# Feed-forward token blocks of 512 and 256 in place of 464 and 448, with x at another address

## The chip, the core and the metric

The kernel is one program on one core of a Trainium2 chip. The metric is the device time of one execution in microseconds (us), as the median of three runs. Beside it stands one execution that the hardware profiler recorded, with its own time and its span from the first to the last instruction.

## What is computed

Causal attention with a decay, on 4 batches of 8 heads with 576 positions and 64 features each, gives an array x of 2304 tokens by 512 features. Two feed-forward parts follow, both over all tokens:

```python
x = attention(q, k, v, f)            # 2304 tokens x 512
h = x @ moe_w_in                     # 512 -> 2048
x = (h * sigmoid(h)) @ moe_w_out     # 2048 -> 512
a, b = x @ moe2_w_a, x @ moe2_w_b    # 512 -> 1536, twice
out = (a * b) @ moe2_w_out           # 1536 -> 512
```

Inputs and output are float32.

## The kernel before

The program has two stretches. In the first, a planner (class `Plan`) orders the attention of 16 head pairs together with the first piece of the first feed-forward part, by hand-given durations and priorities; `first_chunk` is that piece, in token blocks of 288 columns (`NB`). Nothing in it reads `BLOCKS`.

The second stretch, the loops at the end of `model_kernel`, is the rest of both feed-forward parts. `chunk_layout` cuts the hidden features into 13 pieces, called chunks: `CH1` holds seven for the first part, `CH2` six for the second, with 1 to 3 tiles of 128 hidden features each. Chunk 0 is the one done in the first stretch; chunks 1 to 12 run here. For each chunk the loop goes over the token blocks of `BLOCKS`: four of 464 and one of 448.

- `ff_in(c, t, t0, n)` makes the hidden tile t for the n tokens from t0. `project` multiplies four 128-feature pieces of x (index kc) by the weights into one PSUM tile `ps`; in the second part there are two such tiles, for a and for b. ScalarE and VectorE turn it into g and split g into a high part `ghi` (line 342) and a low part `glo` (line 343).
- `ff_out(c, oc, t0, n)` multiplies `ghi` and `glo` by the second weights into a PSUM tile `po` and adds that to the accumulator `acc` (`add_out`, lines 364 and 373). The accumulator is held in two halves of 1152 tokens (`TAIL`), so the block that lies across token 1152 is added in two pieces.
- Every product is done by `mm3` as three matmuls with float32r operands (lines 310, 311, 312): high by high, high by low, low by high. The moving operand is a row of n columns of x or of g; the stationary operand is a 128 x 128 piece of the weights, loaded anew for each matmul.
- The loop writes `ff_in` of a block, then `ff_out` of the block before it. A scheduler of the framework sets the final order of the instructions on each engine from its own model.
- Meanwhile the weights of the next chunk are decoded (`decode`, lines 272 to 281) in pieces of 256 columns, three pieces (`PER`) after each token block: a load on SP, six passes on ScalarE and VectorE, two on GpSimd.
- In the last chunk `add_out` issues the output's DMA (line 375) after each add.

x is one tile of 128 partitions, [P, 2, KC, NT] float32r: index 0 of the second axis is the high part, 1 the low part, KC is 4, NT is 2304. In the built kernel it begins at byte 20,768 of each partition, which is 81 x 256 + 32. A step of kc is 9,216 bytes and from high to low 36,864 bytes, both multiples of 256, so what a block's read begins at, modulo 256, is (32 + 4 t0) modulo 256: 32, 96, 160 and 224 for the blocks at tokens 0, 464, 928 and 1392, and 32 for the one at 1856. It is set by the small tiles that stand ahead of x in a partition, of which `warm` ([NH, 1], 4 bytes, line 247) is the last: it only takes the result of an early Exp.

Of the kernel before, what the change touches and what calls it, by code (L numbers as in the profile page):

```python
# [9 lines left out]
F32 = mybir.dt.float32  # L10
# [3 lines left out]
AF = mybir.ActivationFunctionType  # L14
# [6 lines left out]
NT, DM = B * S, H * D  # L21
KC = DM // P
FF1, FF2 = 2048, 1536
NH = B * H
# [15 lines left out]


TAIL = NT // 2
BLOCKS = [(t, min(464, NT - t)) for t in range(0, NT, 464)]

# [183 lines left out]
def model_kernel(ctx: ExitStack, tc: tile.TileContext, qk, q0, v, f, w, out):  # L230
    nc = tc.nc
    chunks, _ = chunk_layout()

    const = ctx.enter_context(tc.tile_pool(name="const", bufs=1))
# [9 lines left out]
    dec = dram.tile([NH, 6, 2, S], BF16, name="dec")  # L244

    invs = dram.tile([NH // 2, 9, P], F32, name="invs")
    warm = const.tile([NH, 1], F32, name="warm")
    temp = ExitStack()
    dp = temp.enter_context(tc.tile_pool(name="dp", bufs=1))
    ft, one, cum = (dp.tile([NH, S], F32, name=n) for n in ("ft", "one", "cum"))  # L250
# [65 lines left out]
    gp = [None, 0, 0]  # L316
# [74 lines left out]
    plan = Plan()  # L391
# [3 lines left out]
    def buf(pool, tag, shape, dtype, name):  # L395
        n = SLOTS[tag]
        return Buf(tags[tag], lambda: (pool or dpool[0]).tile(shape, dtype, name=name, tag=tag, bufs=n))
# [6 lines left out]
    def prepare():  # L404

        pr = -9
        for n, (t, base, fill, op) in enumerate(((maskb, 0.0, MASKED, ALU.is_ge), (ident, 1.0, 0.0, ALU.is_equal))):
            plan.add("POOL", 142, lambda t=t, base=base: nc.gpsimd.memset(t, base), (), [("const", n)], -10)
            plan.add("POOL", 244, lambda t=t, fill=fill, op=op: nc.gpsimd.affine_select(
                t, t, pattern=[[-1, P]], compare_op=op, fill=fill, base=0, channel_multiplier=1), (), [("const", n)], -10)  # L410
        plan.add("DVE", 135, lambda: nc.vector.tensor_copy(identb, ident), [("const", 1)], [("const", 2)], pr)

        idle = warmth.append(buf(mm, "mm", [P, 512], F32, "idle")) or warmth[0]

        def run_up():
            for n in range(RUN_UP):
                nc.tensor.matmul(idle()[:, :P], identb, maskb, start=n == 0, stop=n == RUN_UP - 1)

        plan.add("PE", 6000, run_up, [("const", 0), ("const", 2)], [idle], pr)
        plan.dma(480, 74000, lambda: nc.sync.dma_start(ft, f), (), ["f"], pr)  # L420
        plan.add("DVE", 607, lambda: nc.vector.memset(one, 1.0), (), ["one"], pr)
        plan.add("DVE", 369, lambda: nc.vector.tensor_scalar(ft, ft, 1e-4, 1.0, ALU.max, ALU.min), (), ["f"], pr)
        plan.add("ACT", 1900, lambda: nc.scalar.activation(ft, ft, AF.Ln), (), ["f"], pr)

        plan.add("ACT", 1400, lambda: nc.scalar.activation(warm, one[:, 0:1], AF.Exp), ["one", "f"], ["warm"], pr)
        plan.add("DVE", 669, lambda: nc.vector.tensor_tensor_scan(cum, one, ft, 0.0, ALU.mult, ALU.add), ["f", "one"], ["cum"], pr)
        plan.add("POOL", 133, lambda: nc.gpsimd.tensor_copy(warm, cum[:, 0:1]), ["cum"], ["warm", "go"], pr)
        plan.add("DVE", 400, lambda: nc.vector.memset(maskw, 0.0), ["cum"], [("const", 3)], -7)
        plan.add("DVE", 250, lambda: nc.vector.memset(mask2, 0.0), ["cum"], [("const", 3)], -7)
        plan.add("POOL", 250, lambda: nc.gpsimd.tensor_copy(maskw[:, -P:], maskb), [("const", 0), "cum"], [("const", 3)], -7)  # L430
        for i in range(2):
            plan.add("POOL", 100, lambda i=i: nc.gpsimd.tensor_copy(mask2[i * D:(i + 1) * D, -D:], maskb[:D, :D]),
                     [("const", 0), "cum"], [("const", 3)], -7)
        for i, value in enumerate((-1 / SCALE, 1 / SCALE)):
            plan.add("POOL", 1200, lambda i=i, value=value: nc.gpsimd.memset(rows_sb[:, 3 - 3 * i:6 - 3 * i, i], value), ["cum"], [("rows", "const", i)], -8)
        rest = (ft, one)
        for n in range(3):
            src = cum if n == 0 else rest[n - 1]
            plan.add("DVE", 450, lambda n=n, src=src: nc.vector.tensor_copy(rows_sb[:, n, 0], src), [("c", n), "cum"], [("rows", n)], -8)
            if n < 2:  # L440
                plan.add("DVE", 750, lambda n=n, src=src: nc.vector.tensor_sub(rest[n], src, rows_sb[:, n, 0]),
                         [("c", n), ("rows", n), "cum"], [("c", n + 1), ("f", "one")[n]], -8)
        for n in range(3):
            plan.add("ACT", 530, lambda n=n: nc.scalar.copy(rows_sb[:, 3 + n, 1], rows_sb[:, n, 0]), [("rows", n)], [("rows", "k", n)], -8)
        plan.dma(480, 442000, lambda: nc.scalar.dma_start(dec, rows_sb), [("rows", n) for n in range(3)] + [("rows", "k", n) for n in range(3)] + [("rows", "const", i) for i in range(2)],
                 ["dec"], pr, eng="ACT")
# [338 lines left out]
    def keep_warm(order):  # L785
# [10 lines left out]
        return res  # L796

    prepare()
    fill_decays()

# [45 lines left out]


    mmpool[0] = ctx.enter_context(tc.tile_pool(name="mmB", bufs=8, space=PSUM))
    gp[:] = ctx.enter_context(tc.tile_pool(name="gB", bufs=2)), 3, 464
    prev = []  # L850
    for c in range(1, len(chunks)):
        pend = []
        for t0, nb in BLOCKS:
            for t in range(chunks[c][2]):
# [55 lines left out]
```

## Time and profile before

| what | value |
|---|---|
| median of 3 runs | 1052.15 us (1051.17 to 1052.24) |
| the profiled execution | 1050.7 us, of it a span of 1049.0 us |
| granted TensorE clock, mean | 0.996 of full speed |
| matmuls in the span | 5814 |
| of them in chunks 1 to 12 | 3840 (2280 on x, 1560 on g) |
| columns in one pass over the tokens | 2304 |

The page of a profile gives each engine's busy time (PE is TensorE's matmuls, PEld its weight loads, DVE is VectorE, ACT ScalarE, POOL GpSimd, SP SyncE). A matmul's row has its start and a duration; durations of matmuls that follow each other overlap, so what one costs is read from start to start. The timeline lists instructions by start; the chain of waits follows the work that ended last back from the end.

### The profile page before, as it was taken

What the parts mean: (1) busy time and instruction counts of PE and PEld (TensorE: products, weight loads), DVE (VectorE), ACT (ScalarE), POOL (GpSimd) and SP (SyncE); (2) the same over time, 40 slices, a digit from 0 to 9 for tenths busy, and PEclk for the clock granted to TensorE, in tenths of its full rate; (3) what the DMA queues carried; (4) which work ended last, traced back from release to release, by engine and by line L of the source; (5) the groups of instructions that cost most, each with busy time, mean ns of one, the idle gap of its engine ahead of it and who ended that gap; (6) DMA issues with size and microseconds to landing.
All of it is one profiled execution on the core that took longest, in us unless ns stands there. A gap on an engine that the chain in (4) does not pass through costs nothing.

```text
span 1049.0 us, 16188 instructions
## 1 busy us (share of the span) xinstructions
PE 1034.1 (99%) x5814; PEld 900.1 (86%) x5814; DVE 650.6 (62%) x1545; ACT 438.6 (42%) x1074; POOL 325.9 (31%) x353
## 2 busy tenths in 40 slices
PE   8989999999999999999999999999999999999998
PEld 7757777888889899898898988988989888989987
DVE  8886555469887756846548965176475475473333
ACT  7888878854343323323225544332232231331110
POOL 5563433134333303304007762151141250340000
PEclk9999999999999999999999999999999999999999
DMA  5443331122121201201001212021021021010013
GB/s 164 151 137 116 118 104 56 40 75 71 52 81 33 88 11 41 81 1 51 31 1 57 65 57 65 1 72 51 1 81 41 21 71 31 21 60 1 28 46 108
DMA packets 34096, 62.35 MB, mean 59 GB/s; under 512 B 7004, under 2 KB 10220, under 8 KB 33984
## 3 DMA queue, kind: packets, MB, share of 16 engines
q1 hardware_dynamic: 33904, 60.87, 18.0%
q8 instruction: 46, 0.75, 0.3%
q10 hardware_dynamic: 112, 0.45, 0.2%
q14 instruction: 34, 0.28, 0.1%
HBM read 56.05 MB, written 5.23 MB: 58 GB/s over the span
## 4 chain that ended last, share of the span: by engine, by line
PE 94%; DVE 3%; ACT 1%; issue 1%; DMA 1%; POOL 0%; ACTq 0%; DVEq 0%; POOLq 0%
PE ps L310 15%; PE ps L311 15%; PE ps L312 15%; PE po L310 10%; PE po L311 10%; PE po L312 10%; PE s L558 4%; PE pv L678 3%; PE t_y L634 2%; PE t_x L634 2%; DVE p L584 1%; PE po L754 1%; PE ps L754 1%; PE po L755 1%; PE po L756 1%; PE ps L755 1%
## 5 line engine op out<-in xcount | busy, mean ns | idle before, releaser
L310 PE MATMUL ps<-x,whi 128*128 128x464 f32 (+1 forms) x760 | 282.8, 372 | 0.5 <-ACT acc L782 0.5
L311 PE MATMUL ps<-x,whi 128*128 128x464 f32 (+1 forms) x760 | 282.8, 372 | 0.0
L312 PE MATMUL ps<-x,wlo 128*128 128x464 f32 (+1 forms) x760 | 282.8, 372 | 0.0
L280 POOL TENSOR_TENSOR d<-d,whi 128x256 f32<-128x256 f32 x124 | 104.4, 850 | 436.4 <-ACT whi L279 436.2
L311 PE MATMUL po<-glo,whi 128*128 128x464 f32 (+1 forms) x520 | 192.5, 370 | 0.0
L312 PE MATMUL po<-ghi,wlo 128*128 128x464 f32 (+1 forms) x520 | 192.0, 369 | 0.0
L310 PE MATMUL po<-ghi,whi 128*128 128x464 f32 (+1 forms) x520 | 191.0, 371 | 0.0
L310 PEld LDWEIGHTS ps<-x,whi 128*128 128x128 f32 x760 | 142.7, 188 | 17.7 <-ACT acc L782 0.8
L312 PEld LDWEIGHTS ps<-x,wlo 128*128 128x128 f32 x760 | 142.6, 188 | 17.0
L311 PEld LDWEIGHTS ps<-x,whi 128*128 128x128 f32 x760 | 142.6, 188 | 16.8
L342 ACT CAST ghi<-g 128x464 fp32r<-128x464 f32 (+1 forms) x130 | 75.0, 577 | 155.5 <-DVE g L341 93.8
L272 ACT ACTIVATE d<-d 128x256 f32<-128x256 f32 x124 | 53.0, 434 | 141.7 <-DMA d<-in_w 130.7
L281 POOL TENSOR_TENSOR wlo<-d,d 128x256 fp32r<-128x256 f32 x124 | 99.7, 812 | 34.7 <-DVE d L278 33.5
L341 DVE TENSOR_TENSOR g<-g,ps 128x464 f32<-128x464 f32 (+1 forms) x60 | 37.8, 630 | 114.2 <-PE ps L312 114.2
L343 DVE TENSOR_TENSOR glo<-g,ghi 128x464 fp32r<-128x464 f32 (+1 forms) x130 | 89.8, 691 | 29.7 <-ACT ghi L342 29.2
L312 PEld LDWEIGHTS po<-ghi,wlo 128*128 128x128 f32 x520 | 97.7, 188 | 10.8
L310 PEld LDWEIGHTS po<-ghi,whi 128*128 128x128 f32 x520 | 97.7, 188 | 10.5
L311 PEld LDWEIGHTS po<-glo,whi 128*128 128x128 f32 x520 | 97.7, 188 | 10.2
L273 DVE TENSOR_SCALAR d<-d 128x256 uint32<-128x256 uint32 x124 | 46.0, 374 | 76.8 <-ACT d L272 75.6
L364 DVE SCALAR_TENSOR_TENSOR acc<-po,acc 128x464 f32<-128x464 f32 (+3 forms) x144 | 75.1, 549 | 27.6 <-PE po L312 27.5
L373 DVE TENSOR_TENSOR acc<-po,acc 128x464 f32<-128x464 f32 (+2 forms) x120 | 63.8, 552 | 26.0 <-PE po L312 25.3
L279 ACT CAST whi<-d 128x256 fp32r<-128x256 f32 x124 | 48.6, 403 | 65.5 <-DVE d L274 36.6
(121 smaller groups left out, 1440.0 us busy)
## 6 DMA issues: line engine op xcount, KB each, us to landing
d<-in_w SPq DMA_DIRECT2D x128, 256.0 KB
qk<-in_qk SPq DMA_DIRECT2D x15, 608.0 KB
vt<-in_v SPq DMA_DIRECT2D x16, 320.0 KB
rb<-invs SPq DMA_DIRECT2D x32, 128.0 KB
out_t<-acc SPq DMA_DIRECT2D x12, 232.0 KB
d2ghi<-in_w SPq DMA_DIRECT2D x8, 256.0 KB
out_t<-acc SPq DMA_DIRECT2D x4, 224.0 KB
whole<-in_q SPq DMA_DIRECT2D x2, 288.0 KB
```

The source lines that it names most:

```text
L272: nc.scalar.activation(m, high.bitcast(F32), AF.Copy, scale=2.0 ** -112)
L273: nc.vector.tensor_scalar(m.bitcast(U32), m.bitcast(U32), 3, None, ALU.logical_shift_left)
L279: nc.scalar.copy(hi, val)
L280: nc.gpsimd.tensor_sub(m, val, hi.bitcast(F32))
L281: nc.gpsimd.tensor_add(lo, m, e)
L310: nc.tensor.matmul(ps, wh, mh, start=start, stop=False)
L311: nc.tensor.matmul(ps, wh, ml, start=False, stop=False)
L312: nc.tensor.matmul(ps, wl, mh, start=False, stop=stop)
L342: nc.scalar.copy(ghi[:, t, :n], g)
L343: nc.vector.tensor_sub(glo[:, t, :n], g, ghi[:, t, :n].bitcast(F32))
L364: nc.vector.scalar_tensor_tensor(a, ps, 0.5, a, ALU.mult, ALU.add)
L373: nc.vector.tensor_add(a, ps, a)
```

## The change

Three lines set it. The token blocks become four of 512 and one of 256, at tokens 0, 512, 1024, 1536 and 2048; the pool of g makes its tiles 512 wide; and `warm` becomes 64 floats wide, of which the first is used as before. With that x begins at byte 20,992, which is 82 x 256. All tiles allocated behind x move by the same 224 bytes or more: the accumulators, the weights of chunks 1 to 12 and the tiles of g then begin at multiples of 256 too. Tiles of the attention and of chunk 0's weights and g lie at the other end of the memory and do not move. The block that lies across token 1152 is now 1024 to 1535, added in pieces of 128 and 384.

```diff
-BLOCKS = [(t, min(464, NT - t)) for t in range(0, NT, 464)]
+BLOCKS = [(t, min(512, NT - t)) for t in range(0, NT, 512)]
...
-    warm = const.tile([NH, 1], F32, name="warm")
+    warm = const.tile([NH, 64], F32, name="warm")
...
-        plan.add("ACT", 1400, lambda: nc.scalar.activation(warm, one[:, 0:1], AF.Exp), ["one", "f"], ["warm"], pr)
+        plan.add("ACT", 1400, lambda: nc.scalar.activation(warm[:, 0:1], one[:, 0:1], AF.Exp), ["one", "f"], ["warm"], pr)
...
-        plan.add("POOL", 133, lambda: nc.gpsimd.tensor_copy(warm, cum[:, 0:1]), ["cum"], ["warm", "go"], pr)
+        plan.add("POOL", 133, lambda: nc.gpsimd.tensor_copy(warm[:, 0:1], cum[:, 0:1]), ["cum"], ["warm", "go"], pr)
...
-    gp[:] = ctx.enter_context(tc.tile_pool(name="gB", bufs=2)), 3, 464
+    gp[:] = ctx.enter_context(tc.tile_pool(name="gB", bufs=2)), 3, 512
```

The order of the instructions stays nearly the same; their widths change. On PE, in chunk 2 (two hidden tiles), the end of the last block's `ff_in` and the start of the `ff_out` of the block before it. Names are ps_chunk_which_tile_t0 and po_chunk_oc_t0; the last number is the buffer's. Before:

```order
L310 MATMUL ps_2_0_1_1856_4431<-x_289,whi2_3723 128x448
L311 MATMUL ps_2_0_1_1856_4431<-x_289,whi2_3723 128x448
L312 MATMUL ps_2_0_1_1856_4431<-x_289,wlo2_3724 128x448
L310 MATMUL po_2_0_1392_4448<-ghi_2_1392_4297,whi2_3723 128x464
L311 MATMUL po_2_0_1392_4448<-glo_2_1392_4298,whi2_3723 128x464
L312 MATMUL po_2_0_1392_4448<-ghi_2_1392_4297,wlo2_3724 128x464
```

and with the change:

```order
L310 MATMUL ps_2_0_1_2048_4431<-x_289,whi2_3723 128x256
L311 MATMUL ps_2_0_1_2048_4431<-x_289,whi2_3723 128x256
L312 MATMUL ps_2_0_1_2048_4431<-x_289,wlo2_3724 128x256
L310 MATMUL po_2_0_1536_4448<-ghi_2_1536_4297,whi2_3723 128x512
L311 MATMUL po_2_0_1536_4448<-glo_2_1536_4298,whi2_3723 128x512
L312 MATMUL po_2_0_1536_4448<-ghi_2_1536_4297,wlo2_3724 128x512
```

The order is the same, but the 24 matmuls of the last block's `ff_in`, of which three are shown, are 256 columns wide instead of 448, while the products behind them, which need g of the block before, are 512 wide instead of 464.

On DVE, in the same chunk, the instructions from g of that earlier block's second hidden tile to its `glo`. Before:

```order
L338 SCALAR_TENSOR_TENSOR g_2_1_1392_4317<-g_2_1_1392_4317,ps_2_0_1_1392_4318 128x464
L364 SCALAR_TENSOR_TENSOR acc_290<-po_2_0_928_4335,acc_290 128x224
L364 SCALAR_TENSOR_TENSOR acc1_3403<-po_2_0_928_4335,acc1_3403 128x240
L276 TENSOR_SCALAR d2_3_2560_4399<-d3_3_2560_4400 128x256
L364 SCALAR_TENSOR_TENSOR acc_290<-po_2_1_928_4344,acc_290 128x224
L364 SCALAR_TENSOR_TENSOR acc1_3403<-po_2_1_928_4344,acc1_3403 128x240
L343 TENSOR_TENSOR glo_2_1392_4298<-g_2_1_1392_4317,ghi_2_1392_4297 128x464
```

and with the change:

```order
L338 SCALAR_TENSOR_TENSOR g_2_1_1536_4317<-g_2_1_1536_4317,ps_2_0_1_1536_4318 128x512
L364 SCALAR_TENSOR_TENSOR acc_290<-po_2_0_1024_4335,acc_290 128x128
L364 SCALAR_TENSOR_TENSOR acc1_3403<-po_2_0_1024_4335,acc1_3403 128x384
L276 TENSOR_SCALAR d2_3_2816_4482<-d3_3_2816_4483 128x256
L364 SCALAR_TENSOR_TENSOR acc_290<-po_2_1_1024_4344,acc_290 128x128
L364 SCALAR_TENSOR_TENSOR acc1_3403<-po_2_1_1024_4344,acc1_3403 128x384
L343 TENSOR_TENSOR glo_2_1536_4298<-g_2_1_1536_4317,ghi_2_1536_4297 128x512
```

The same seven instructions stand between the two, with 512 columns for 464 in the first and the last, and 128 and 384 for 224 and 240 in the adds.

## Rows read from the trace of the kernel before

**Rows 1.** The page: PE's busy time and share of the span.
```profile
PE 1034.1 (99%) x5814; PEld 900.1 (86%) x5814; DVE 650.6 (62%) x1545; ACT 438.6 (42%) x1074; POOL 325.9 (31%) x353
```
**Rows 2.** The page, the chain that ended last: shares by engine.
```profile
PE 94%; DVE 3%; ACT 1%; issue 1%; DMA 1%; POOL 0%; ACTq 0%; DVEq 0%; POOLq 0%
```
**Rows 3.** Waits of PE: the only one behind the first stretch.
```profile
PE ps L310 <- ACT acc L782: 0.5, 1, 0.5
```
**Rows 4.** The page's groups: high by high matmuls on x, on g.
```profile
L310 PE MATMUL ps<-x,whi 128*128 128x464 f32 (+1 forms) x760 | 282.8, 372 | 0.5 <-ACT acc L782 0.5
...
L310 PE MATMUL po<-ghi,whi 128*128 128x464 f32 (+1 forms) x520 | 191.0, 371 | 0.0
```
**Rows 5.** Timeline of PE: first and last matmul of chunks 1 to 12.
```profile
241.81 0.48 PE L310 MATMUL ps<-x,whi 128*128 128x464 f32 x1 [0.50 <-ACT acc L782]
...
1044.92 0.37 PE L312 MATMUL po<-ghi,wlo 128*128 128x448 f32 x1
```
**Rows 6.** Timeline of PE, chunk 12: first matmul of each part (start, duration, us).
```profile
964.79 0.37 PE L310 MATMUL ps<-x,whi 128*128 128x464 f32 x1
...
974.87 0.36 PE L310 MATMUL po<-ghi,whi 128*128 128x448 f32 x1
...
979.75 0.37 PE L310 MATMUL ps<-x,whi 128*128 128x464 f32 x1
...
989.83 0.37 PE L310 MATMUL po<-ghi,whi 128*128 128x464 f32 x1
...
994.84 0.37 PE L310 MATMUL ps<-x,whi 128*128 128x464 f32 x1
...
1005.07 0.38 PE L310 MATMUL po<-ghi,whi 128*128 128x464 f32 x1
...
1010.11 0.37 PE L310 MATMUL ps<-x,whi 128*128 128x464 f32 x1
...
1020.33 0.37 PE L310 MATMUL po<-ghi,whi 128*128 128x464 f32 x1
...
1025.35 0.36 PE L310 MATMUL ps<-x,whi 128*128 128x448 f32 x1
...
1035.26 0.37 PE L310 MATMUL po<-ghi,whi 128*128 128x464 f32 x1
...
1040.27 0.36 PE L310 MATMUL po<-ghi,whi 128*128 128x448 f32 x1
```
**Rows 7.** Windows over the block at token 928, chunks 8 and 12: engines' busy us (instructions), PEclk.
```profile
693.40:703.70 10.30, 10.30 (x50) 9.04 (x50) 6.33 (x16) 3.49 (x9) 3.63 (x5) 1.00 0.24 75
994.80:1005.10 10.30, 10.30 (x50) 9.04 (x50) 1.92 (x3) 1.67 (x3) 0.00 (x0) 1.00 0.12 46
```
**Rows 8.** Timeline of PE in chunk 0: 24 matmuls of 288 columns, first and next.
```profile
215.68 0.29 PE L754 MATMUL ps<-x,whi 128*128 128x288 f32 x1
...
218.85 0.36 PE L754 MATMUL po<-ghi,whi 128*128 128x288 f32 x1
```
**Rows 9.** The chain near the start: bf16 matmuls of 128 columns (start, us).
```profile
8.39 1.06 PE idle L793 x19
```
**Rows 10.** Timelines of PE and DVE in chunk 2, around the last two blocks.
```profile
302.29 0.36 PE L310 MATMUL ps<-x,whi 128*128 128x448 f32 x1
...
305.37 0.62 DVE L343 TENSOR_TENSOR glo<-g,ghi 128x464 fp32r<-128x464 f32 x1
...
307.24 0.38 PE L310 MATMUL po<-ghi,whi 128*128 128x464 f32 x1
```
**Rows 11.** Timelines of ACT and PE in chunk 1: ghi of block 1392, its use.
```profile
259.74 0.58 ACT L342 CAST ghi<-g 128x464 fp32r<-128x464 f32 x1 [1.87 <-DVE g L338]
...
262.00 0.58 PE L310 MATMUL po<-ghi,whi 128*128 128x464 f32 x2
```
**Rows 12.** Timeline of DVE: the last add, and adds of 224 columns (two).
```profile
1045.33 0.62 DVE L373 TENSOR_TENSOR acc<-po,acc 128x448 f32<-128x448 f32 x1 [0.60 <-PE po L312]
...
303.84 0.69 DVE L364 SCALAR_TENSOR_TENSOR acc<-po,acc 128x224 f32<-128x224 f32 x2
```

## The prediction

> **What bounds the kernel now.** I read the page's busy times first: PE is busy for 1034.1 of 1049.0 us [rows 1], and the chain that ended last is 94% PE [rows 2]. Then the waits: in chunks 1 to 12 PE waits once, for 0.5 us [rows 3]. So this stretch, which is all that the change touches, is as long as its matmuls follow each other. They run from 241.81 to 1044.92 us plus the last one's 0.2 us, 803.3 us for 3840 matmuls [rows 5], at a granted clock of 1.00, which is 2.4 GHz [rows 7]. What a reader should take from these rows: a matmul's own 372 ns [rows 4] is not its price, since the next one starts 209 ns later. Only starts count here.
>
> **Spacings.** The columns alone would take 768 weight tiles x 2304 columns / 2.4 GHz = 737.3 us. The other 66 us are 17 ns per matmul that its columns don't explain, and they are the whole matter of this change: neither the number of matmuls (five blocks before and after) nor that of columns changes. In chunk 12 each part's starts give the spacing [rows 6]. On x, 48 matmuls each: token block 0 10.08 us or 210.0 ns, 464 the same 210.0, 928 213.1, 1392 212.9, and the 448 columns at 1856 206.5. On g, 24 each: 208.8, 210.0, 209.2 and 208.8 ns at 464 columns, and 202.2 at 448 (4.65 us for 23). One pass over the tokens, five blocks, is thus 1052.5 ns on x and 1038.9 on g. With 760 x 3 / 5 = 456 such passes on x and 312 on g [rows 4] that makes 804.1 us, within 0.1% of the measured 803.3, so chunk 12 speaks for all.
>
> Two things in these numbers decide what I expect. First, other engines are not the cause: the block at 928 has 50 matmuls in 10.30 us both where DVE is busy for 6.33 us and where it is for 1.92 [rows 7]. Second, the address seems to be part of it: blocks on x that begin at remainder 32 or 96 of 256 bytes take 210.0 ns, those at 160 and 224 take 213, at the same width. The excess also grows with the width: 24 matmuls of 288 columns take 3.17 us, 132.1 ns each [rows 8], 12 ns over their columns where 464 columns have 16 to 20.
>
> **The change, term by term.**
>
> *Wider and narrower matmuls at remainder 0.* Every block on x and every tile of g, and the weights, now begin at multiples of 256 bytes. The trace has no float32r matmul of 512 or of 256 columns on 128 rows, and none whose moving operand begins there, so this price is bounded. The upper end is the dear state of tokens 928 and 1392: a line through 132.1 ns at 288 and 213.0 at 464 (0.460 ns a column) gives 235.1 ns at 512 and 117.4 at 256, or 1057.8 per pass. The lower end is the bf16 matmuls near the start: 19 in 1.06 us, 55.8 ns for 128 columns [rows 9], 2.5 ns over the columns; the same 2.5 ns gives 215.8 and 109.2, or 972.4 per pass. I take the cheap state of the same operation, since it is the nearest row: the mean of the two cheap blocks on x and the four on g, 209.5 ns at 464, and 132.1 at 288 give 0.440 ns a column, so 230.5 ns at 512 and 118.0 at 256, 1040.0 per pass. On x that is 12.5 ns less x 456 = -5.7 us; on g 1.1 more x 312 = +0.3. Together **-5.4 us**.
>
> *Cover for g.* ff_out needs g of the block before, and what hides the work on g is the last block's ff_in, which shrinks. In chunk 2 that ff_in lasts from 302.29 to 307.24, and glo of the block before is done at 305.99 [rows 10], 3.7 us after that block's last matmul on x. It is needed by the fifth matmul of ff_out, 5.8 us after. Now there are 24 x 0.118 + 4 x 0.2305 = 3.75 us, while the work on g grows by a tenth of its wide pieces to some 3.95. That is 0.2 us of waiting, in chunk 2 and in chunk 6, which also has two tiles. In chunk 1 ghi is done at 260.32 [rows 11], 3.3 us after the block's matmuls end at 257.06, and used at 262.00; now after 12 x 0.2305 + 12 x 0.118 = 4.2 us, still in time. Longer chunks have more cover. I take +0.5 us, with 0 and 3 as ends: if DVE falls behind on its queue of decode passes, PE waits there and the tanh and adds queued behind it come late too.
>
> *The end.* The last add covers 256 columns for 448. It took 0.62 us, and 224 columns take 0.35 [rows 12], so some 0.24 us go. The last output DMA carries 128 KB for 224, and the 3.05 us from the last add's end to the span's end hold it: nothing to 0.5 us. I take -0.4 in all.
>
> *At no cost.* The wider `warm` is written in one column as before. Decode keeps its 256-column pieces, and POOL and SP hold the same work beside PE. In chunk 0, 192 matmuls on x start at remainders 0 and 128 instead of 32 and 160; by the cheap line they cost the same, by the bf16 row 1.8 us less.
>
> **The sum.** 1050.7 - 5.4 + 0.5 - 0.4 = 1045.4 us against the profiled execution. The median of the runs is 1.45 us above that execution, so 1046.9, say **1047 us**. Its own range, from the ends of the smaller terms, is 1043 to 1050.
>
> **Rivals.**
>
> *Reads at multiples of 256 bytes run at the columns' rate.* The excess falls to 2.5 ns, as in the bf16 row: (80.1 x 456 + 66.5 x 312) = -57.3 us, with the other terms 1050.7 - 57.3 + 0.1 - 1.8 = 991.7, or 993 us as a median. For it: the excess depends on the address [rows 6], all float32r reads of this trace begin at 32 modulo 64, and the bf16 operands of rows 9 begin at multiples of 64. Against it: bf16 moves half the bytes per column, so those rows don't show that address is the reason. The Trainium skill, TensorE: Matmul & The Clock Gate, section "Wait — 56ns, not 53.3ns?", puts the spacing of warm back-to-back matmuls at N / 2.4 + about 2.5 ns, 215.7 at 512 columns; by that rule alone the stretch would take 746.9 us. Here the trace differs, with 209 to 213 ns at 464, so either the rule leaves out float32r or address explains the rest.
>
> *Remainder 0 is a dear address.* Everything now begins at one remainder, moving and stationary operand alike. If that is the state of tokens 928 and 1392, x costs 5.3 ns more per pass x 456 = 2.4 us, and g, now mostly cheap, 18.9 x 312 = 5.9: +8.3, so 1059 us profiled and 1060.5 as a median. The place is the 512-column matmul; from 232.2 ns on (where a pass with 118.0 for the narrow block equals today's mean of 1047.0) the change loses. For it: two of four remainders tried on x are dear. Against it: the dear ones begin in the upper half of their 256 bytes, and 0 does not.
>
> *Address is immaterial.* The excess goes by columns, and these don't change: 1050.8, or 1052 as a median; the 213 ns blocks would then come from something else, and come back. The Trainium skill, SBUF — State Buffer, section "Specifications (TRN2)", gives lines of 16 bytes, with a penalty for each access that crosses to a new one. By that rule this is the outcome, since all starts were multiples of 16 already; that blocks of one width differ by 3 ns speaks against it being the whole story.
>
> **How the numbers follow.** The forecast has 0.38, full rate 0.28, the dear address 0.22, immaterial 0.12. A measurement of this kernel tells a difference from none at about 0.2%, 2.1 us. Faster: forecast and full rate, 0.66, and 0.01 from the edge of the last case; within 0.2%: 0.11; slower 0.22. The range takes in full rate with 3 us to spare and leaves out the upper half of the dear case: 990 to 1058. Times in between, where part of the excess goes, are in it.
>
> **What would show it.** The spacing of 512-column matmuls in chunk 12: near 230 ns is my case, 216 full rate, 235 the dear address, and a mix of spacings at one width would say that start addresses alone don't set it. 256 columns should take 118 ns. PE's waits on ACT or DVE at the last block of chunks 2 and 6 should be under 1 us. I am wrong if the 512-column spacing is under 227 or over 232 ns, or if PE waits for more than 3 us in chunks 1 to 12.

## The result, and the profile after

The changed kernel takes **1039.94 us** (median of 4 runs, 1039.84 to 1040.95) where the kernel before took 1052.16 us beside it (4 runs): a ratio of 0.989, 95% interval 0.9878 to 0.9902, 12.2 us less. The profiled execution took 1039.84 us with a span of 1038.1 us, 10.9 less than the span before. The forecast was 1047 us, some 5 us less than before: the sign was right, the size less than half of what came.

The page of the changed kernel: busy times [rows 1], shares of the chain that ended last [rows 2], and the groups of high by high matmuls [rows 4].

```profile
PE 1021.1 (98%) x5814; PEld 847.8 (82%) x5814; DVE 658.8 (63%) x1545; ACT 441.5 (43%) x1074; POOL 324.5 (31%) x353
...
PE 85%; DVE 6%; DMA 2%; ACT 1%; issue 1%; POOL 0%; ACTq 0%; DVEq 0%; SPq 0%; POOLq 0%
...
L310 PE MATMUL ps<-x,whi 128*128 128x512 f32 (+1 forms) x760 | 279.8, 368 | 1.5 <-ACT acc L782 1.2
...
L310 PE MATMUL po<-ghi,whi 128*128 128x512 f32 (+1 forms) x520 | 190.0, 368 | 0.6 <-ACT ghi L342 0.6
```

The matmuls' own durations hardly changed (368 ns for 372), and PE is still busy nearly always. What changed is how soon the next one starts. PE's timeline shows it: the first matmul of chunk 1, then the first of each part of chunk 12 from the block at token 1024 on, then the last matmul (start, duration in us), as in [rows 5, 6].

```profile
243.16 0.50 PE L310 MATMUL ps<-x,whi 128*128 128x512 f32 x1 [1.23 <-ACT acc L782]
...
988.00 0.39 PE L310 MATMUL ps<-x,whi 128*128 128x512 f32 x1
...
998.88 0.39 PE L310 MATMUL po<-ghi,whi 128*128 128x512 f32 x1
...
1004.32 0.39 PE L310 MATMUL ps<-x,whi 128*128 128x512 f32 x1
...
1015.20 0.39 PE L310 MATMUL po<-ghi,whi 128*128 128x512 f32 x1
...
1020.64 0.28 PE L310 MATMUL ps<-x,whi 128*128 128x256 f32 x1
...
1026.39 0.40 PE L310 MATMUL po<-ghi,whi 128*128 128x512 f32 x1
...
1034.61 0.28 PE L312 MATMUL po<-ghi,wlo 128*128 128x256 f32 x1
```

On x, 48 matmuls of 512 columns take 10.88 us (988.00 to 998.88), **226.7 ns** each, and on g 24 take 5.44, 226.7 again; the mean over all chunks and blocks on x is 226.9. The 256-column ones take 5.75 / 48 = 119.8 ns. These are 13.3 and 13.1 ns over their columns at 2.4 GHz (213.3 and 106.7), called 13.3 from here on, where 464 columns had 16 to 20. From the first start to the last are 791.45 us, where there were 803.11 [rows 5]: **11.7 us less**.

The rest of the difference in span is small and of both signs. The first matmul of chunk 1 starts 1.35 us later than before, most of which is not the change's doing: the same changed kernel, profiled again (e16 below), had it at 242.08. From the last matmul's start to the end of the span are 3.49 us for 4.08. Together -11.7 + 1.35 - 0.6 = -10.9, the difference of the spans.

Of the 11.7 us, the spacings give more and waits take some back. The means of all spacings in chunks 1 to 12, without those over 300 ns, add up on x to 1027.4 ns for a pass over the five blocks, for 1050.3 before, and on g to 1027.8 for 1039.1. That is 22.9 x 456 + 11.3 x 312 = 14.0 us less. Seven spacings over 300 ns hold 2.5 us more than 227 ns each, where before there was one with 0.1. PE's waits name them [rows 3]:

```profile
PE ps L310 <- ACT acc L782: 1.2, 1, 1.2
...
PE po L310 <- ACT ghi L342: 0.6, 1, 0.6
PE po L311 <- DVE glo L343: 0.6, 1, 0.6
...
PE ps L310 <- DVE acc L364: 0.2, 1, 0.2
```

The first is the start of chunk 1. The two of 0.6 are in chunk 6, the one of 0.2 at the start of chunk 2. By the starts, 1.77 us are lost in chunk 6 and 0.6 between chunks 1 and 2; the latter comes and goes (0.1 in e16, the same kernel).

### The profile page after: what moved, and what is told of

The parts are those of the page before. It is cut to its first block, busy times and chain, and to the rows that moved or that the text cites. A ratio compares the mean times of both kernels' runs of the same rounds, so it can differ in the third digit from the quotient of the medians.

```text
span 1038.1 us, 16146 instructions
## 1 busy us (share of the span) xinstructions
PE 1021.1 (98%) x5814; PEld 847.8 (82%) x5814; DVE 658.8 (63%) x1545; ACT 441.5 (43%) x1074; POOL 324.5 (31%) x353
## 4 chain that ended last, share of the span: by engine, by line
PE 85%; DVE 6%; DMA 2%; ACT 1%; issue 1%; POOL 0%; ACTq 0%; DVEq 0%; SPq 0%; POOLq 0%
PE ps L310 14%; PE ps L312 14%; PE ps L311 14%; PE po L311 10%; PE po L312 9%; PE po L310 9%; PE s L558 4%; PE pv L678 3%; PE t_y L634 2%; DMA d<-in_w 2%; PE t_x L634 2%; PE ps L754 1%; DVE acc L364 1%; PE po L754 1%; PE ps L755 1%
## 5 line engine op out<-in xcount | busy, mean ns | idle before, releaser
L310 PE MATMUL ps<-x,whi 128*128 128x512 f32 (+1 forms) x760 | 279.8, 368 | 1.5 <-ACT acc L782 1.2
L311 PE MATMUL ps<-x,whi 128*128 128x512 f32 (+1 forms) x760 | 279.7, 368 | 0.0
L312 PE MATMUL ps<-x,wlo 128*128 128x512 f32 (+1 forms) x760 | 279.5, 368 | 0.0
L311 PE MATMUL po<-glo,whi 128*128 128x512 f32 (+1 forms) x520 | 191.6, 368 | 0.6 <-DVE glo L343 0.6
L312 PE MATMUL po<-ghi,wlo 128*128 128x512 f32 (+1 forms) x520 | 191.3, 368 | 0.0
L310 PE MATMUL po<-ghi,whi 128*128 128x512 f32 (+1 forms) x520 | 190.0, 368 | 0.6 <-ACT ghi L342 0.6
L342 ACT CAST ghi<-g 128x512 fp32r<-128x512 f32 (+1 forms) x130 | 75.1, 578 | 147.1 <-DVE g L341 95.2
L341 DVE TENSOR_TENSOR g<-g,ps 128x512 f32<-128x512 f32 (+1 forms) x60 | 37.9, 632 | 116.2 <-PE ps L312 115.7
L343 DVE TENSOR_TENSOR glo<-g,ghi 128x512 fp32r<-128x512 f32 (+1 forms) x130 | 89.3, 687 | 34.1 <-ACT ghi L342 33.5
L364 DVE SCALAR_TENSOR_TENSOR acc<-po,acc 128x512 f32<-128x512 f32 (+3 forms) x144 | 75.8, 551 | 23.2 <-PE po L312 22.9
L373 DVE TENSOR_TENSOR acc<-po,acc 128x512 f32<-128x512 f32 (+2 forms) x120 | 64.6, 554 | 25.5 <-PE po L312 25.0
```

The lines of the kernel that those rows point to most:

```text
L310: nc.tensor.matmul(ps, wh, mh, start=start, stop=False)
L311: nc.tensor.matmul(ps, wh, ml, start=False, stop=False)
L312: nc.tensor.matmul(ps, wl, mh, start=False, stop=stop)
L342: nc.scalar.copy(ghi[:, t, :n], g)
L343: nc.vector.tensor_sub(glo[:, t, :n], g, ghi[:, t, :n].bitcast(F32))
L364: nc.vector.scalar_tensor_tensor(a, ps, 0.5, a, ALU.mult, ALU.add)
```

## The experiments

Sixteen more runs were made; e5 to e8, e13 and e14 are one profiled execution each, and are used for their spacings. "Stretch" is the time from the first to the last matmul start of chunks 1 to 12 in the profiled execution.

### Widths or address: e1 to e3

e1 keeps 464 and 448 and takes only the 64-float tile, so x, weights and g begin at multiples of 256 bytes. e2 takes only the widths, and e3 puts x at remainder 64.

```diff
# e1, against the changed kernel
-BLOCKS = [(t, min(512, NT - t)) for t in range(0, NT, 512)]
+BLOCKS = [(t, min(464, NT - t)) for t in range(0, NT, 464)]
...
-    gp[:] = ctx.enter_context(tc.tile_pool(name="gB", bufs=2)), 3, 512
+    gp[:] = ctx.enter_context(tc.tile_pool(name="gB", bufs=2)), 3, 464
# e2
-    warm = const.tile([NH, 64], F32, name="warm")
+    warm = const.tile([NH, 1], F32, name="warm")
# e3
-    warm = const.tile([NH, 64], F32, name="warm")
+    warm = const.tile([NH, 16], F32, name="warm")
```

> Only the address part of the change: x, the weights and g placed as in the changed kernel, but token blocks of 464 and 448 as before, so reads begin at remainders 0, 64, 128 and 192 of 256 bytes. Theory A (a multiple of 64 bytes is enough; a matmul then costs its columns plus 13.3 ns): every block at 206.7 ns (464) or 200.0 ns (448), chunks 1 to 12 in 788.5 us, no waits of PE there as before, so about 1036 us, below both kernels. Theory B (only multiples of 256 help): the block at token 0 and the one at 1856 at 206.7 and 200.0 ns, those at 464, 928 and 1392 at 210 to 213, about 1046 us. Theory C (the widths do it, not the address): 209 to 213 ns as before, about 1051 us.

> Only the block part of the change: blocks of 512 and 256, warm one float wide, so x, the weights and g begin at remainder 32 of 256 bytes. Theories A and B (addresses do it): the 512-column spacing is 229 to 232 ns instead of the 226.7 of the changed kernel, chunks 1 to 12 take about 801 to 806 us, and the time is 1050 to 1056 us. Theory C (the widths do it): 226.7 ns and about 1040 us.

> As the changed kernel, but warm 16 floats wide: x, the weights and g all begin at remainder 64 of 256 bytes. Theory A (multiples of 64 are enough): 226.7 ns at 512 columns, 119.7 at 256, and 1040 us. Theory B (256 is needed): over 229 ns and 1049 us or more. Theory C (widths): 1040 us.

| kernel | median, us | ratio to before, 95% interval | stretch, us |
|---|---|---|---|
| e1, address alone | 1051.71 | 1.000, 0.999 to 1.0009 | 803.2 |
| e2, widths alone | 1039.60 | 0.9885, 0.9868 to 0.9901 | 791.6 |
| e3, widths, x at 64 | 1039.32 | 0.9883, 0.9868 to 0.9898 | 792.1 |

The address alone is worth nothing and the widths alone are worth all of it. Chunk 12 of e1, blocks at tokens 464 and 928, whose reads of x now begin at 64 and 128:

```profile
979.89 0.37 PE L310 MATMUL ps<-x,whi 128*128 128x464 f32 x1
...
989.97 0.37 PE L310 MATMUL po<-ghi,whi 128*128 128x464 f32 x1
...
994.98 0.37 PE L310 MATMUL ps<-x,whi 128*128 128x464 f32 x1
...
1005.21 0.38 PE L310 MATMUL po<-ghi,whi 128*128 128x464 f32 x1
```

10.08 and 10.23 us for 48 matmuls: 210.0 and 213.1 ns, what [rows 6] showed at 96 and 160. In e2, where everything begins at remainder 32, the spacings are the changed kernel's: 226.9 and 119.8 ns on x, the mean of all.

### Does the start ever count: e5 and e9

e5 puts x alone 128 bytes further at 464 columns, which exchanges the blocks' halves; e9 puts x, weights and g of the changed kernel into the upper half of their 256 bytes.

```diff
# e5, against e1
-    warm = const.tile([NH, 64], F32, name="warm")
+    warm = const.tile([NH, 32], F32, name="warm")
...
         accs[0] = pool.tile([P, KC, TAIL], F32, name="acc")
+        pool.tile([P, 32], F32, name="pad")
# e9, against the changed kernel
-    warm = const.tile([NH, 64], F32, name="warm")
+    warm = const.tile([NH, 32], F32, name="warm")
```

> Blocks of 464 and 448, with x alone moved to remainder 128 of 256 bytes (weights and g stay at multiples of 256 or 64), so the reads of the blocks at tokens 0, 464, 928 and 1392 begin at 128, 192, 0 and 64. If the dear blocks are those that begin in the upper half of 256 bytes, they swap: 213 ns at tokens 0 and 464, 210 at 928 and 1392. If the address does nothing at all, the blocks keep their spacings: 209 to 210 ns at 0 and 464, 213 at 928 and 1392, and the time stays at 1052 us.

> The changed kernel with the small tile ahead of x 32 floats wide, so that x, the weights and the tiles of g begin in the upper half of their 256 bytes (remainder 128). At 464 columns blocks that begin there took 213 ns and others 210. Theory C, the widths set the spacing and at 512 and 256 columns the start is immaterial: 226.7 and 120.0 ns and 1040 us. Rival, the upper half costs the same 3 ns at 512 columns too, and the starts tried so far (0, 32 and 64) were all on the cheap side: 230 ns, 768 x 4 x 3.3 = 10 us more, 1050 us.

Chunk 12 of e5, blocks at tokens 464 and 928, now at remainders 192 and 0:

```profile
980.62 0.37 PE L310 MATMUL ps<-x,whi 128*128 128x464 f32 x1
...
990.86 0.37 PE L310 MATMUL po<-ghi,whi 128*128 128x464 f32 x1
...
995.87 0.37 PE L310 MATMUL ps<-x,whi 128*128 128x464 f32 x1
...
1005.95 0.37 PE L310 MATMUL po<-ghi,whi 128*128 128x464 f32 x1
```

213.3 and 210.0 ns: the cheap block and the dear one have changed places with their starts, so at 464 columns the start does set these 3 ns. One profile of e5 took 1051.27 us (before 1050.82 beside it): two blocks are dear wherever x lies, so the sum stays. At 512 columns the start sets nothing: e9 took 1039.16 us (ratio 0.9882, 0.9865 to 0.9898) with 226.7 ns at remainder 128.

### Which widths: e4, e6, e7, e8

```diff
# against the changed kernel, one line each
-BLOCKS = [(t, min(512, NT - t)) for t in range(0, NT, 512)]
+BLOCKS = [(0, 512), (512, 512), (1024, 512), (1536, 384), (1920, 384)]   # e4
+BLOCKS = [(0, 512), (512, 496), (1008, 480), (1488, 464), (1952, 352)]   # e6
+BLOCKS = [(0, 512), (512, 448), (960, 432), (1392, 416), (1808, 496)]    # e7
+BLOCKS = [(0, 512), (512, 512), (1024, 448), (1472, 320), (1792, 512)]   # e8
```

> As the changed kernel, with token blocks of 512, 512, 512, 384 and 384, so the last block gives the work on g more cover. If a matmul costs its columns plus 13.3 ns at any width: 173.3 ns at 384 columns, the same 788 us of matmuls in chunks 1 to 12, and the 2.5 us of PE's waits at the narrow last block of chunks 1, 2 and 6 mostly gone: 1037 to 1038 us. If the excess goes with the columns (13.3 ns per 512): 170 ns at 384 columns, 780 us and 1029 us.

> The changed kernel with blocks of 512, 496, 480, 464 and 352 tokens: a scan of widths. Theory D (only multiples of 128 columns get away with columns plus 13.3 ns): 226.7 ns at 512, and 2 to 7 ns above columns plus 13.3 elsewhere, that is 222 to 227 ns at 496, 215 to 220 at 480, 209 to 213 at 464, 162 to 167 at 352; about 1050 us. Theory E (multiples of 64 are enough) gives the same for these widths. If the width isn't it and the 464 spacings come from the blocks' order, all widths have 13.3: 220.0, 213.3, 206.7, 160.0 ns and 1039 us.

> The changed kernel with blocks of 512, 448, 432, 416 and 496 tokens. Theory D: 448 at 202 to 207 ns, 432 at 195 to 200, 416 at 189 to 194, 496 at 222 to 227; about 1050 us. Theory E: 448 at 200.0 ns, the other three as in D; 1048 us. If the width isn't it: 200.0, 193.3, 186.7, 220.0 ns and 1039 us.

> The changed kernel with blocks of 512, 512, 448, 320 and 512 tokens: odd multiples of 64 beside 512. Theory D: 448 at 202 to 207 ns and 320 at 149 to 154 ns; 1041 to 1044 us. Theory E: 200.0 and 146.7 ns, and 1039 us.

e4 took 1040.58 us (ratio 0.9893, 0.9879 to 0.9908), so two blocks of 384 are nearly as good as 512 and 256. The 1037 to 1038 us that its expectation gave did not come: PE's waits did not go but stand at 0.9 us in chunk 6 and 0.5 in chunk 7. e6, e7 and e8 took 1046.06, 1046.77 and 1043.14 us in one profiled execution each; 2.8 us of e8 and 0.9 of e7 are waits of PE on ScalarE in chunk 7, so the widths are compared by spacings. Chunk 12 of e7, the blocks of 448, 416 and 496 columns on x:

```profile
977.23 0.36 PE L310 MATMUL ps<-x,whi 128*128 128x448 f32 x1
...
986.96 0.39 PE L310 MATMUL po<-ghi,whi 128*128 128x512 f32 x1
...
1006.69 0.35 PE L310 MATMUL ps<-x,whi 128*128 128x416 f32 x1
...
1015.65 0.36 PE L310 MATMUL po<-ghi,whi 128*128 128x432 f32 x1
...
1020.36 0.39 PE L310 MATMUL ps<-x,whi 128*128 128x496 f32 x1
...
1031.23 0.35 PE L310 MATMUL po<-ghi,whi 128*128 128x416 f32 x1
```

For 48 matmuls 9.73, 8.96 and 10.87 us: 202.7, 186.7 and 226.5 ns, which is 16.0, 13.4 and 19.8 over the columns. 496 columns at this start cost what 512 do. All widths on x (mean spacing of all chunks minus columns / 2.4; remainder of the start in brackets):

| columns | ns over the columns |
|---|---|
| 512, 384, 320, 256 (0; 512 and 256 also 32, 64, 128) | 13 to 14.5 |
| 496 | 13.4 (0), 19.8 (64) |
| 480 | 16.0 (192) |
| 464 | 16 (0, 32), 17 (64, 96), 19 to 20 (128 to 224) |
| 448 | 16 (0 in e7 and e8), 18.2 (0 in e1, 32 before), 17.2 (128) |
| 432 | 15.8 (0) |
| 416 | 13.4 (192) |
| 352 | 19.8 (128) |

So some 13 ns is the least in this table (the 288 columns of chunk 0 had 12.1 [rows 8]), and some widths pay 2.5 to 6.5 ns more, how much also by their start. Theories D and E both fail: 320, 416 and, at 0, 496 columns pay no more than 512, so multiples of 128 aren't needed, and 448 pays though it is a multiple of 64. Nor is it a matter of wide or narrow.

Start and width aren't all, either. In the kernel before, the block of 448 at token 1856 behaves in two ways at one start. PE's timeline has it so in chunk 11, the 448 columns on x and then the first matmul of the next part; chunk 12 is in [rows 6]:

```profile
950.05 0.37 PE L310 MATMUL ps<-x,whi 128*128 128x448 f32 x1
...
959.78 0.37 PE L310 MATMUL po<-ghi,whi 128*128 128x464 f32 x1
```

That is 9.73 us for 48, 202.7 ns, against 9.91 or 206.4 in chunk 12. Chunks 1, 4, 7, 9 and 11 have 202.6 to 202.9 and the others 206.1 to 206.5, in e1 as well, so 18.2 in the table is the mean of two states. The blocks of 464 at 160 have 210.5 and 210.9 ns in chunks 1 and 4 and 213 in the rest. What puts a chunk into one state or the other was not tried.

### What the 13.3 ns are: e11, e13, e14

In e11 the middle one of three matmuls has 64 stationary columns for 128; in e13 and e14 all but the first and last of a PSUM tile do, at 512 and 256 columns and at 464 and 448. These products are left out for half of the outputs, so less is written to PSUM too, and not only less loaded.

```diff
# e11
-        nc.tensor.matmul(ps, wh, ml, start=False, stop=False)
+        nc.tensor.matmul(ps[:64], wh[:, :64], ml, start=False, stop=False)
# e13, and e14 on top of e1
-        nc.tensor.matmul(ps, wh, mh, start=start, stop=False)
-        nc.tensor.matmul(ps, wh, ml, start=False, stop=False)
-        nc.tensor.matmul(ps, wl, mh, start=False, stop=stop)
+        h = slice(0, P if start else 64)
+        nc.tensor.matmul(ps[h], wh[:, h], mh, start=start, stop=False)
+        nc.tensor.matmul(ps[:64], wh[:, :64], ml, start=False, stop=False)
+        h = slice(0, P if stop else 64)
+        nc.tensor.matmul(ps[h], wl[:, h], mh, start=False, stop=stop)
```

> In chunks 1 to 12 the middle one of each three matmuls (high weights by low data) has 64 of its 128 stationary columns; the correction is left out for half of the outputs. The moving operand, its width and the number of matmuls stay. Theory L, the 13.3 ns over the columns are the loading of the 128 stationary columns for each matmul, a quarter of a 2.4 GHz cycle for each: one in three spacings falls by 6.7 ns, to 220.0 ns at 512 and 113.3 ns at 256, 1280 x 5 / 5 x 6.7 = 8.5 us less, 1031.5 us. Theory F, a fixed price per matmul whatever it loads: 226.7 and 120.0 ns in all three places, 1040 us.

> The changed kernel, but in chunks 1 to 12 all matmuls except the first and the last of each PSUM tile have 64 of their 128 stationary columns; those products are left out for half of the outputs. So 10 of 12 matmuls on x follow each other with loads of half the size. Theory L, the 13.3 ns are the load's 128 columns at a quarter of a cycle each: 220.0 ns at 512 columns and 113.3 at 256 in these runs. Theory F, a fixed price: 226.7 and 120.0. Theory P, loads and data get in each other's way in a repeating pattern that load sizes and widths set together, as the run with one load in three halved suggests (229.8 and 116.9 on average): neither value, and different signs at 512 and at 256.

> The same halved loads with blocks of 464 and 448 columns at the aligned start, where full loads gave 209.4, 210.0 and 213.0 ns, 2.7 to 6.3 ns over the columns plus 13.3. Theory L: 464 columns fall to 200.0 ns if the extra goes with the load, or to some 203 to 206 if only half of the 13.3 does. Theory F: 209 to 213 as before. Theory P: the extra takes another value at each start, so the order of cheap and dear starts (0 and 64 cheap, 128 and 192 dear) does not hold any more.

e11 took 1044.96 us (ratio 0.9939, 0.9925 to 0.9954), slower than the changed kernel with less to load: 512 columns 229.8 ns on average, 256 columns 116.8. Chunk 12 of e13, the block at token 1024 and the narrow one (the matmul's line is now 311):

```profile
990.72 0.39 PE L311 MATMUL ps<-x,whi 128*128 128x512 f32 x1
...
1001.74 0.39 PE L311 MATMUL po<-ghi,whi 128*128 128x512 f32 x1
...
1023.74 0.28 PE L311 MATMUL ps<-x,whi 128*128 128x256 f32 x1
...
1029.25 0.39 PE L311 MATMUL po<-ghi,whi 128*128 128x512 f32 x1
```

The narrow block takes 5.51 us for 48, and between two half loads most spacings are 113 and 114 ns, 6.7 over the columns: half the load, half the excess, as theory L has it. But at 512 columns it is 11.02 us, 229.6 ns, 3 ns more than with full loads; theory L fails there. Between half loads the spacings run through a cycle of six (224, 227, 234, 230, 236, 229). In e14, between half loads, 464 columns take 210.4, 208.4, 209.5 and 209.4 ns at 0, 64, 128 and 192, so the cheap and the dear half are gone. Theory P, which foretold different signs at 512 and 256 columns and another order of the starts, fits; that loads and data get in each other's way is argued by it, not shown.

### The waits: e10, e12, e15, e16

```diff
# e10
-BLOCKS = [(t, min(512, NT - t)) for t in range(0, NT, 512)]
+BLOCKS = [(0, 512), (512, 512), (1024, 256), (1280, 512), (1792, 512)]
# e12, and e15
-    W0, W1, PER = 256, 256, 3
+    W0, W1, PER = 256, 256, 4
# e15 only
-        for t0, nb in BLOCKS:
+        for t0, nb in (BLOCKS if c != 6 else [(0, 256)] + [(t, 512) for t in range(256, NT, 512)]):
```

> The changed kernel with the block of 256 tokens in the middle (at token 1024) and not at the end. Widths and starts are the same, so 226.7 and 120.0 ns. In the changed kernel PE loses some 2.5 us to waits in chunks 1 to 12, of it 1.8 us in chunk 6 behind the narrow block. Theory W, what makes these long is the work that ScalarE and VectorE do at the end of a chunk (the first part's last block is turned into x there): in the middle the waits fall under 1 us and the time to 1038 us. Rival, the cover is short wherever the narrow block stands, since its input products are half as long: the waits move to chunks 1, 2 and 6 behind token 1024 and stay at 2 to 4 us, 1040 to 1041 us.

> The changed kernel with four pieces of the next chunk's weights decoded after each token block and not three, so that the twelve pieces are behind the first three blocks and VectorE and ScalarE hold none when g of block 1536 is made. In the changed kernel PE loses 1.8 us in chunk 6 to that g, and 2.5 us in all. Theory D, the decode's passes ahead of it on VectorE are what makes g late: the waits at the narrow block go, 1038 us (1.2 to 2 us less). Rival, the pieces only come earlier, VectorE falls behind in the blocks before, PE waits there instead, and where it waits for over 2 us at a time its clock falls to 0.5 as it did in the run with the narrow block in the middle (16 spacings of 427 ns, 3.2 us more): 1041 to 1044 us.

> Four pieces decoded after each block (as in the run before), and in chunk 6 alone the narrow block comes first (tokens 0 to 255), the other four of 512 behind it. Theory R, g of a 512 block is late in chunk 6 because what hides it is a narrow block's input products (2.9 us) at a place where VectorE's decode passes of 256 columns take 0.8 us for 0.3 beside GpSimd's work on x; with a 512 block in that place, whose input products take 5.4 us, the 1.7 us of waits in chunk 6 go: chunks 1 to 12 last 789 to 789.5 us, and the time is 1036.5 us. Rival, the narrow block takes the wait along to the start of chunk 6, where it hides g of the last block of chunk 5 (three tiles): 1 to 3 us of waits there, and 1038 to 1040 us.

> The changed kernel again, as the comparison for the run beside it on one chip: 1039 to 1041 us, with 1.7 us of waits in chunk 6 and some 0.7 us between chunks 1 and 2.

In the changed kernel chunk 6 looks so on PE, at the end of the narrow block's input products, on DVE (the first row is one of chunk 2, for comparison) and, in the last row, on POOL:

```profile
580.86 0.40 PE L310 MATMUL po<-ghi,whi 128*128 128x512 f32 x1
...
582.33 0.50 PE L310 MATMUL po<-ghi,whi 128*128 128x512 f32 x1 [0.61 <-ACT ghi L342]
583.43 0.50 PE L311 MATMUL po<-glo,whi 128*128 128x512 f32 x1 [0.61 <-DVE glo L343]
```

```profile
308.86 0.28 DVE L276 TENSOR_SCALAR d<-d 128x256 uint32<-128x256 uint32 x1
...
578.18 0.83 DVE L276 TENSOR_SCALAR d<-d 128x256 uint32<-128x256 uint32 x1
...
580.95 0.68 DVE L338 SCALAR_TENSOR_TENSOR g<-g,ps 128x512 f32<-128x512 f32 x1
...
582.54 0.84 DVE L343 TENSOR_TENSOR glo<-g,ghi 128x512 fp32r<-128x512 f32 x1
...
578.04 0.81 POOL L280 TENSOR_TENSOR d<-d,whi 128x256 f32<-128x256 f32 x1 [0.87 <-ACT whi L279]
```

A decode pass that takes 0.28 us in chunk 2 (the first row) takes 0.83 here, beside a pass of the decode on GpSimd. Of the 121 such passes behind 241 us, the 62 with GpSimd idle take 0.28 to 0.30 us, and the 32 that take longer all run beside work of GpSimd; but 27 beside such work take 0.30 or less, so that isn't all of it. g of block 1536's second tile waits in the queue behind such passes until 580.95, and its glo is done at 583.38. Seen from the starts, the spacings of these po matmuls are 1.00 and 1.11 us, and 0.34 for the next, instead of 0.227: 1.77 us lost.

e12 was meant to take the passes away. It took 1038.35 us (ratio 0.988, 0.9864 to 0.9897); in chunk 6 spacings of 0.95 and 1.11 us stand as before, because the scheduler left as many passes on VectorE there (eight between 576 and 584 us in either kernel). So this theory D, of the decode's passes, was not tried as meant. e15 keeps the four pieces and puts a wide block in that place too, and the wait is gone:

```profile
PE ps L310 <- ACT acc L782: 1.3, 1, 1.3
PE ps L310 <- DVE acc L364: 0.2, 1, 0.2
```

That is all that PE waits for behind 241 us. The stretch is 789.59 us where e16, the changed kernel beside it, has 790.90; the medians are 1037.62 (1036.6 to 1037.72; ratio 0.986, 0.9844 to 0.9877) and 1038.73 (1038.2 to 1039.21; ratio 0.9874, 0.9859 to 0.9889). Their ranges don't touch, the intervals of their ratios overlap: e15 is the best of these kernels, by about 1 us.

e10 shows that a wide block there isn't enough by itself, and what such a wait can grow to. With the narrow block in the middle it took 1043.07 us (1040.92 to 1043.57; ratio 0.9916, 0.9901 to 0.9931), 3 us more than the changed kernel. Its timeline of PE in chunk 6, from the first input product of its last block on, and its windows there (engines' busy us, then PEclk):

```profile
571.19 0.40 PE L310 MATMUL ps<-x,whi 128*128 128x512 f32 x1
...
578.09 0.50 PE L310 MATMUL po<-ghi,whi 128*128 128x512 f32 x1 [0.59 <-ACT ghi L342]
580.62 0.80 PE L311 MATMUL po<-glo,whi 128*128 128x512 f32 x1 [2.03 <-DVE glo L343]
581.22 0.63 PE L312 MATMUL po<-ghi,wlo 128*128 128x512 f32 x1
581.64 0.63 PE L310 MATMUL po<-ghi,whi 128*128 128x512 f32 x1
...
586.76 0.41 PE L310 MATMUL po<-ghi,whi 128*128 128x512 f32 x1
```

```profile
575.00:577.00 2.00, 2.00 (x11) 1.65 (x10) 2.00 (x7) 1.62 (x5) 1.20 (x2) 1.00 0.01 3
577.00:581.20 4.20, 1.58 (x5) 0.76 (x4) 4.20 (x12) 3.13 (x10) 3.90 (x8) 0.85 0.19 62
581.20:586.70 5.50, 5.50 (x14) 4.29 (x13) 5.08 (x10) 1.96 (x4) 3.83 (x6) 0.50 0.30 86
```

The products that wait are those of block 1280, and ahead of them stand 24 input products of 512 columns (from 571.19 on): the wait isn't behind the narrow block. What delays glo here is VectorE's queue: between 577.30 and 579.61 it holds two decode passes and six adds of 128 columns of the narrow block. So a wide block in the last place waits with three pieces (e10), a narrow one waits with four (e12), and the wide one with four doesn't (e15); which part of e15's order does it was not separated.

Three starts of PE come 3.4 us late in all, 2.6 us of it waits. While PE stands, the granted clock falls to 0.50 (1.2 GHz), and 13 matmuls (not 16, as the expectation of e12 counts them) take from 581.22 to 586.76, 426 ns each. Each loses 0.2 us, 2.6 us in all: the waiting is paid nearly twice. Not every run of e10 does so: the profiled one and one more have a mean granted clock of 0.993, the other two 0.997 (1043.57 and 1040.92 us). In the changed kernel the spacings of 1.00 and 1.11 us left the clock at 1.00, and so did e8's waits of 1.5 and 1.3 us.

## Why the prediction missed the size

**What bounds the kernel: right.** The stretch is as long as its matmuls follow each other, starts are the price and durations aren't. Spacings in a block don't depend on the other engines' load: the block at 1024 takes 10.88 us with DVE busy for 8.19 and for 2.07 us, as [rows 7] had it.

```profile
692.16:703.04 10.88, 10.88 (x49) 9.01 (x48) 8.19 (x19) 4.14 (x10) 6.39 (x8) 1.00 0.28 85
988.00:998.88 10.88, 10.88 (x49) 9.01 (x48) 2.07 (x3) 1.80 (x3) 0.00 (x0) 1.00 0.12 48
```

**The spacing term failed: -5.4 us forecast, -14.0 measured.** The step is "0.440 ns a column", the line through 132.1 ns at 288 columns and 209.5 at 464, drawn on to 512. It rests on "the excess also grows with the width". It doesn't: it falls from 16 to 20 ns at 464 to 13.3 at 512, and is the same 13.3 at 256. The true values, 226.7 and 119.8, lie inside the bounds that I gave (215.8 to 235.1 and 109.2 to 117.4) for the wide block, and outside them for the narrow one, where the steeper line's 117.4 was no upper end: my own 118.0 lies above it. The sum's own range, 1043 to 1050, took in the ends of the smaller terms only and nothing for this one, the largest. On x the term was -5.7 and came to -10.4; on g +0.3 and came to -3.5. Chunk 12 did not quite speak for all: its pass on x took 1052.5 ns, the mean of all chunks 1050.3, since its block of 448 is in the dearer of its two states. My sign that I was wrong, a spacing under 227, was met. The rows of before already spoke against a line: at one remainder, 32, the 448 columns of token 1856 had 206.5 ns, 19.8 over their columns, and the 464 of token 0 had 16.7 [rows 6]. What they couldn't show is that both are dear widths: at 13.3 ns over the columns the old blocks would take as long as the new ones, 768 x (2304 / 2.4 + 5 x 13.3) = 788.4 us, and the old stretch took 14.7 us more than that.

**The reason was wrong too.** I tied the excess to the address. At 464 columns the start does count (e1, e5), by 3 ns between the halves of 256 bytes, but moving x moves no time (e1: ratio 1.000), and at 512 no start tried counts (e2, e3, e9). The whole gain is the widths'. So the right sign owes much to luck: it came from putting every block on x into the cheap state of an address. The same line through the mean of the four wide blocks on x, 211.5 ns, gives 1050.3 for a pass, and -1.0 us in place of -5.7.

**Cover for g: +0.5 us forecast, 2.4 measured**, inside the 0 to 3. Chunk 6 was named and has 1.77 of it; chunk 2 was named and has 0.05, and 0.6 came between chunks 1 and 2, where I expected none. What I mis-sized is the work on g, "grows by a tenth": I took it from chunk 2, and in chunk 6 VectorE's passes take up to three times as long. Chunk 2's rows were misread besides: 302.29 [rows 10] is where the last block's `ff_in` starts, not where block 1392's products on x end. The last of these in PE's timeline of the kernel before:

```profile
297.06 0.38 PE L312 MATMUL ps<-x,wlo 128*128 128x464 f32 x1
```

Behind it come 24 products of `ff_out` and only then the `ff_in`, so glo was done 8.7 us after the block's products and not 3.7, and both parts are cover for it.

**The end: -0.4 forecast, -0.6 measured.** **At no cost**: it fits; the 1.35 us by which chunk 1 starts later differ between runs of one kernel too (1.1 of it between the two profiles of the changed kernel). Chunk 0's products on x went from 132 to 133 ns at their new starts, 0.2 us for all 192.

**The rivals.** Full rate at multiples of 256 bytes (993 us) would have had 216 ns: no. The rule of the Trainium skill beside it, TensorE: Matmul & The Clock Gate, section "Wait — 56ns, not 53.3ns?", N / 2.4 + about 2.5 ns, has the right form for 512 and 256 columns, a constant that doesn't grow with the width; the constant measured for these float32r matmuls is 13.3, and 464 or 448 columns keep to no one constant. The dear address (1060.5 us) would have had 235 ns: no. Address immaterial (1052 us): right about the address of the new blocks, wrong that the excess goes by columns.

## What to carry to other kernels

A spacing is the columns' time plus something that needn't grow with the columns, so two widths don't make a line for a third: before counting on an untried width, time it. Where a narrow block hides other work, look at that work in the chunk where the other engines are busiest, not in a quiet one. And look at the granted clock behind a wait of TensorE: in e10 waits of 0.6 and 2.0 us in a row were followed by 5.5 us of matmuls at half clock, which cost as much again.

## What the runs showed of the hardware that was not expected

- Float32r matmuls of 512 and of 256 columns with 128 stationary columns follow each other in columns / 2.4 GHz + 13.3 ns, at every start tried. At 256 columns halving the stationary columns halves that (113.3 ns), so there it may well go with the load of the weights; at 512 it makes the spacing longer (229.6 for 226.7), and why stays open.
- The same 448 columns at the same start take 202.7 ns in one chunk and 206.4 in the next (kernel before), each steadily for a whole block.
- Where a width pays more, the spacings repeat in cycles. At 448 columns in e7 five matmuls take 199, 207, 202, 203 and 202 ns, 1013 ns, which is five times 200 (448 / 2.4 + 13.3) plus once 13.3; the dear 464 (213.0 to 213.3) is 206.7 plus half of 13.3. That is arithmetic on the rows; what makes the cycle was not found, so no rule here says which width and start are cheap.
- At 1.2 GHz the excess is gone: 512 columns take 426 to 427 ns (e10), which is 512 / 1.2 = 426.7.
- VectorE's pass L276 takes 0.28 us in chunk 2 and 0.83 in chunk 6 on the same shape; all that take over 0.30 us run beside work of GpSimd.
